# Two key loads on ScalarE's queue, a one-hot copy on GpSimd, and two more units masked by TensorE in a fused block-sparse attention and feed-forward kernel

## The chip, the cores and the metric

The kernel runs on one core of a Trainium2 chip. The metric is the device time of one execution in microseconds (us). Three runs of the kernel before gave 262.12, 262.63 and 263.25, with a median of 262.63. One further execution was recorded by the hardware profiler; it took 262.88, and its trace spans 261.1 from the first instruction to the last. All rows in this document that tell durations come from that one execution.

## The reference

Attention over 4 batches of 8 heads, 768 positions and a head width of 64, with a block mask, and then a feed-forward layer over all 3072 tokens. `rand_blocks` holds three drawn key blocks for each of the 24 query blocks, so the mask depends on an input (`sampled_blocks`) and has to be built on the chip.

```python
scores = scale * np.matmul(q, k.transpose(0, 1, 3, 2))
blk_i, blk_j = pos[:, None] // 32, pos[None, :] // 32
mask = np.abs(blk_i - blk_j) <= 1
mask = mask | (blk_i == 0) | (blk_j == 0) | (blk_i == 23) | (blk_j == 23)
for qb in range(24):
    for kb in sampled_blocks[qb]:
        mask[qb * 32:(qb + 1) * 32, kb * 32:(kb + 1) * 32] = True
scores = np.where(mask, scores, -1000000000.0)
attn = softmax(scores)                       # with a maximum taken off, and 1e-9 in the divisor
x = matmul(attn, v)  ->  (3072, 512)
h = x @ w_in                                 # 512 -> 2048
g = h * (1.0 / (1.0 + np.exp(-beta * h)))    # beta: one number for each of 2048
out = g @ w_out                              # 2048 -> 512
```

## The kernel before

**Units.** Two heads make a pair, so there are 16 pairs, 4 in each batch. A batch's 768 queries are cut into a tile of 256 and a tile of 512. A unit is one pair with one tile: units 0 to 3 are the four pairs of batch 0 with its first 256 queries, units 4 to 7 the same pairs with the other 512, and so on, 32 units in all. `tile_steps` cuts a unit into steps of 1024 scores for each partition: 3 steps where the tile has 256 queries, 6 where it has 512, 144 steps in the program. A step is a set of TensorE matmuls of `kX` (keys) by `qX` (queries) into a double PSUM bank `sc`, one ScalarE exponential of 128x1024 into a buffer `et`, and, for most units, one VectorE product of `et` with the 0/1 mask `mask01` (the function `mk`). Then follow the products with the values (`va`), a reciprocal and a scaling (`xst`), and a turn into `x`, the feed-forward's input.

**The mask.** The numbers of the drawn blocks are loaded into `sb_i32` by a DMA on ScalarE's queue. VectorE makes `mask16` of them (`mb`), one matmul spreads it over the query columns (`mt`), and ScalarE copies it to `mask_q` (`mtc`) and to `shut_qk` as 0 or -30000 (`neg`). Three more matmuls with the one-hot matrix `onehot` give `mask01` (`km`, `kmc`). For the first N_PEMASK = 4 units the mask is put on by TensorE: ahead of each pair of key-query matmuls stand two matmuls of `onehot` by `shut_qk` into the same bank, which put -30000 where a block is shut, and no VectorE product follows. In all other units VectorE multiplies.

**Loads.** Keys, queries and values come by SP's queue as fp32 into staging buffers (`st`, or parts of `g` early on), are cast to fp16 by VectorE or GpSimd (`s16`, `va`), and for batch 0 are turned by TensorE with the identity and copied to `kX` and `qX` by VectorE or ScalarE; later batches are turned by DMA. The keys of pairs 0 and 1 are loaded in parts (`IN_PARTS`), and `BESIDE` names one part that ScalarE's queue issues, behind `sb_i32`. GpSimd issues the loads of the weights, which also cast them.

**Feed-forward.** `hp` is x by w_in, `th` a tanh on ScalarE into `t_sb`, `gm` VectorE's product into `g`, then the output products with w_out. The first and the last 256 tokens and five tiles of 512 between them make seven stages; all but the first use sums and differences of `g` and `w_out` (tiles `s` and `w_mix`) that save one of eight block products.

**Order.** Nothing is scheduled when the kernel is built. Every operation becomes a node with a number, and the table `STEPS` lists all nodes in the order of their emission, each with its engine and its buffer slots; a colon joins two TensorE nodes that run as halves of the array. Each engine works through its own part of that list in order, so a wrong order shows as an engine that waits although other work is ready. Nearly all lines of the profile carry the line of one helper (`Tap.call`, L200), so groups are told apart by their tiles.

Of the kernel before, what the change touches and what calls it, by code (L numbers as in the profile page):

```python
# [11 lines left out]
FP16 = mybir.dt.float16  # L12
# [31 lines left out]
0D 1P0 3A 4P7 8P6 2A 5A 9A 35S4 31S0 32D0 36D1 39S 40D 41P5 49S1 65S4 13S1 33P6 37P1 34A2 42D 6P5  # L44
7A 38D 21S 17S3 25S 96P3 94P1 95Ae 50D1 66G6 14G2 92P0 22D 18G3 26G 45S0 55S2 23P4 15P2 16D1 24D
59S3 10S 43S5 97A0 27P3 19P5 20D 29S4 28A 46G5 53S6 93A1 51P2 80P2 84P3 67P0 47P3 81A3 56G5 73G
82P2 74G 48D0 52D 60D1 68D 57P1 58D3 85A2 44G0 83A5 108P1 109Ac 106P3 107A6 104P2 61P1 62D 30D2
105A4 98P1 99P 116P3 87P0:86 100D0 101D0 117A8 63S7 75G 76G 69S8 54D1 118P1 188P2 189A9 86P 88D4
89D3 120P3 70G6 77G 78G 110P0 111P 112D2 11P4 12D 113D4 64D3 121A1 90P6 197P2 119Aa 194P0 79G
122P1 123P 91D0 124D4 198A3 195Ab 125D3 71P7 72D 191P2 192Ae 114P2 203P0 212P3 213A0 200P2 115D  # L50
190D 196D 201A1 204Aa 215P1 102P7 103D 126P6 127D 214D 193D 199D 149P5 128P4 216Ac 150A2 129A5
137P0 205D 202D 138A0 131P1 140P2 134P3 146P7 143P6 130D1 151D 217D 227P2 141A3 135A1 147A4 144A6
148D 145D 136D 132A5 228A2 218P3 219A4 161P3 167P4 158P5 162A1 168A4 159A2 139D 133D 229D 142D
220D 163D 155P2 224P3 156A3 225Ad 206P0:207 169D 160D 221P2 157D 222A8 226D 207P 244P1 245Ab 208Da
223D 209D4 164P6 173P7 170P4 165A3 246D 152P5 250P0 166D 171A1 174A4 230P1:231 153A0 251A7 175D
247P3 248A6 231P 154D 236S2 239S5 240D0 172D 288P0 232D1 259P2 260A1 256P3 237G3 238S1 233D1 257Ae
242S6 241S 268S7 176P23:182 276P2 277A2 252D 182P 183P:177 279P2 289Ac 285P3 280A5 177P 178P:184
286A3 258D 261D 253P2 271S3 249D 278D 291P0 356D 254Aa 357D 360D 281D 290D 255D 274S8 300S0 282P3
184P 179P 210P4 185P 283A0 292A4 287D 284D 293D 262P0:263 269G1 358D 361D 359D 211A1 180A1 186A0
397P3 412P2 295P1:294 263P 264D3 265D4 398A8 413A9 403P3 294P 243G3 272G2 296D8 297D2 400P2 234P1  # L60
266P0 404Ad 298P2 401A4 235D 406P3 267A 409P2 270S0 303S4 306S1 407A1 299D 410A3 320P2 308P0 329P1
326P3 273S 304G4 311P7 309A3 301G3 402D 321A5 330A6 317P5 362D 405D 399D 363D 327A1 314P6 310D1
331D 322D 275G0 420S5 423S2 426S6 328D 312A0 318A5 319D 315A3 428P0 429A5 341P32:323 434P2 313D
435A6 421G2 323P 414D 316D 430D 411D 431P0 302S2 305S 181S 422S3 324A6 437P3 332P4 325D 335P5
432Aa 424G0 342A2 433D 350P2 333A4 343D 408D 436D 336A5 351A6 338P0 344P1 352D 337D 334D 438A2
339A3 443P1 444Ae 345A4 353P67:347 440P2 441A7 347P 354A1 415P1:416 364D0 445D 451P2 340D 452A0
346D 442D 348A3 439D 416P 454P2 457P0 455Ad 427G1 307G2 417D2 418D3 355D 349D 446P1:447 458Ab
463P2 447P 466P3 464A3 467A2 453D 367D 448Db 449D2 425S 460P0 373P4 461A4 480P1 486P3 370P5:374
487A1 474P0 374P 483P3 456D 465D 365D 459D 368D 462D 481Ac 468D 477P1 482D 475A8 478A7 484A5 371P
# [53 lines left out]
1289D 1181S 1180S 1294A0 1296D 1299P 1301P 1302A1 1300D 1297D 1298D 1303P 1304D 1305P 1306D 1313S  # L123
1312S 1307A 1311D 1308P 1309A 1314S
"""
N_PEMASK = 4
ROWS6 = False
N_XPE = 8
SHUT = 30000.0
# [3 lines left out]
BESIDE = ("k", 1, 2)  # L133
# [100 lines left out]
def kernel(  # L234
# [123 lines left out]
    def emit_first():  # L358
# [4 lines left out]
        for load in beside:  # L363
            load()
# [721 lines left out]
```

## Time and profile before

| | us |
|---|---|
| median of three runs | 262.63 |
| profiled execution, its own time | 262.88 |
| its span | 261.1 |
| TensorE busy | 249.6 (96%) |
| VectorE busy | 226.2 (87%) |
| ScalarE busy | 213.7 (82%) |
| GpSimd busy | 34.8 (13%) |

The span and the busy times come from the page's head. A busy TensorE is not TensorE at its peak: its matmuls are pipelined and the end of each is modelled, so a matmul's row is longer than the time until the next may start. The chain that ended last is counted back from the last instruction; where it names an engine, that engine's own work was what the end waited for. Idle time of an engine stands in brackets behind a row of the timeline, with what ended it.

### The profile page before, as it was taken

To read this page: it belongs to the slowest core of one execution; us is meant where nothing else is said; L and a number is where in the kernel's file an instruction comes from. 1 tells how busy PE (TensorE), PEld (TensorE's weight loads), DVE (VectorE), ACT (ScalarE), POOL (GpSimd) and SP (SyncE) were. 2 spreads that over 40 slices of the span, in tenths; PEclk is the share of its full clock that TensorE was granted. 3 is DMA by queue.
4 is the path that set the end of the run, shared out by engine and by line. 5 is a ranking of instruction groups with operands and counts; after the bars stand their busy time and mean duration, and the time that the engine had idled before them with its cause. 6 is when DMAs were issued, how large, how long until landed. Compare 5 with 4: busy or idle time off the path is not lost.

```text
span 261.1 us, 8802 instructions
## 1 busy us (share of the span) xinstructions
PE 249.6 (96%) x3767; PEld 171.8 (66%) x3767; DVE 226.2 (87%) x445; ACT 213.7 (82%) x288; POOL 34.8 (13%) x50
## 2 busy tenths in 40 slices
PE   5998799999989999999999999999999999999995
PEld 1675575564467976468876457856757986568894
DVE  4366998988999999989999999999999888589683
ACT  5699999999999997899898989975899874675241
POOL 3346001045220005210300200001100000000000
PEclk9999999999999999999999999999999999999999
DMA  6999994969756599931933999460050314100042
GB/s 202 340 342 175 207 198 85 280 167 262 178 194 189 175 121 246 172 133 35 261 83 73 251 147 253 57 137 0 3 183 4 22 23 173 22 3 0 3 160 81
DMA packets 50154, 36.81 MB, mean 141 GB/s; under 512 B 29748, under 2 KB 46660, under 8 KB 50116
## 3 DMA queue, kind: packets, MB, share of 16 engines
q1 hardware_dynamic: 46128, 31.80, 48.8%
q0 software_dynamic: 3680, 4.19, 9.8%
q8 instruction: 29, 0.48, 0.8%
q10 hardware_dynamic: 308, 0.26, 0.3%
q14 instruction: 9, 0.07, 0.1%
HBM read 27.27 MB, written 6.29 MB: 129 GB/s over the span
## 4 chain that ended last, share of the span: by engine, by line
PE 83%; DVE 11%; DMA 1%; ACT 1%; issue 1%; POOL 1%; SPq 0%; DVEq 0%; ACTq 0%
PE sc L200 83%; DVE et L200 5%; DVE g L200 3%; DMA st<-in_k_dram 1%; DVE xst L200 1%; ACT et L200 1%; DVE s L200 1%; DVE recip L200 0%; POOL s L200 0%; POOL va L200 0%; DVE kX L200 0%; ACT t_sb L200 0%; DVE va L200 0%; DVE x L200 0%; SPq L510 0%
## 5 line engine op out<-in xcount | busy, mean ns | idle before, releaser
L200 ACT ACTIVATE et<-sc 128x1024 f16<-128x1024 f32 x144 | 139.8, 1035 | 10.0 <-PE sc L200 8.5
L200 PE MATMUL sc<-x,w_in_sb 128*128 128x512 f16 (+2 forms) x504 | 92.1, 352 | 1.1 <-ACT et L200 0.5
L200 DVE TENSOR_TENSOR et<-et,mask 128x960 f16<-128x960 f16 x132 | 83.2, 670 | 1.4 <-ACT et L200 1.2
L200 ACT ACTIVATE t_sb<-sc,beta_c_sb 128x512 f16<-128x512 f32 (+1 forms) x112 | 65.1, 641 | 21.4 <-PE sc L200 19.4
L200 DVE SCALAR_TENSOR_TENSOR g<-t_sb,sc 128x512 f16<-128x512 f16 (+1 forms) x112 | 63.5, 606 | 7.8 <-ACT t_sb L200 7.3
L200 PEld LDWEIGHTS <-w_in_sb 128*128 128x128 f16 (+1 forms) x504 | 42.9, 97 | 37.5 <-issue 4.7
L200 PEld LDWEIGHTS <-g 64*128 64x128 f16 (+1 forms) x700 | 49.1, 96 | 15.2 <-issue 3.3
L200 PE MATMUL sc<-w_out_sb,g 64*128 64x256 f16 (+3 forms) x568 | 55.6, 281 | 0.5 <-DVE xst L200 0.3
L200 PE MATMUL sc<-qX,kX 64*128 64x256 f16 (+1 forms) x384 | 50.6, 328 | 1.4 <-DVE g L200 0.8
L200 PEld LDWEIGHTS <-et 64*128 64x128 f16 (+1 forms) x1776 | 41.7, 95 | 8.6 <-issue 1.4
L200 PE MATMUL sc<-va,et 64*128 64x65 f16 (+1 forms) x1776 | 44.3, 191 | 0.8 <-DVE xst L200 0.3
L200 PEld LDWEIGHTS <-kX 64*128 64x128 f16 x384 | 19.7, 95 | 12.5 <-issue 7.5
L200 POOL CAST s<-st 128x768 f16<-128x768 f32 (+2 forms) x17 | 15.1, 905 | 87.4 <-PE sc L200 34.5
L200 PEld LDWEIGHTS <-s 64*128 64x128 f16 (+1 forms) x320 | 22.0, 97 | 6.0 <-issue 1.7
L200 PE MATMUL sc<-w_mix,s 64*128 64x256 f16 (+1 forms) x272 | 23.6, 270 | 0.0
L200 DVE TENSOR_TENSOR xst<-sc,recip 128x256 f16<-128x256 f32 (+1 forms) x32 | 17.8, 557 | 0.9
L200 POOL CAST va<-st 128x768 f16<-128x768 f32 x10 | 9.6, 968 | 59.0 <-DVE g L200 32.0
L200 ACT COPY osb<-sc 128x512 f32<-128x512 f32 (+3 forms) x19 | 10.0, 539 | 8.5 <-PE sc L200 7.5
L200 PE MATMUL sc<-w_mix,g 64*128 64x256 f16 (+3 forms) x128 | 15.6, 264 | 0.0
L200 DVE TENSOR_TENSOR osb<-osb,sc 128x512 f32<-128x512 f32 (+2 forms) x19 | 11.7, 618 | 2.6 <-PE sc L200 1.5
L200 DVE RECIPROCAL recip<-sc 128x4 f32<-128x4 f32 (+1 forms) x32 | 6.2, 193 | 8.0 <-PE sc L200 7.7
L200 DVE CAST s<-st 128x768 f16<-128x768 f32 (+2 forms) x15 | 7.7, 522 | 2.0 <-DMA st<-in_k_dram 2.0
(60 smaller groups left out, 94.8 us busy)
## 6 DMA issues: line engine op xcount, KB each, us to landing
out_dram<-osb SPq DMA_DIRECT2D x23, 256.0 KB, 2.4
st<-in_k_dram SPq DMA_DIRECT2D x12, 384.0 KB, 4.9
st<-in_q_dram SPq DMA_DIRECT2D x12, 384.0 KB, 5.1
st<-in_v_dram SPq DMA_DIRECT2D x12, 384.0 KB, 4.5
g<-in_v_dram SPq DMA_DIRECT2D x4, 384.0 KB, 6.9
w_in_sb<-in_moe_w_in_dram POOLq DMA_DIRECT2D x2, 512.0 KB, 7.1
w_in_sb<-in_moe_w_in_dram POOLq DMA_DIRECT2D x1, 1024.0 KB, 10.7
w_out_sb<-in_moe_w_out_dram POOLq DMA_DIRECT2D x2, 512.0 KB, 12.9
```

The costliest lines, as they stand in the source:

```text
L200: r = f(*a, **kw)
```

## The change

Four things are changed by hand, and then `STEPS` is replaced as a whole.

First, `BESIDE` now names two loads, the first third of the keys of pair 1 and of pair 0. ScalarE's queue issues the one of pair 1 ahead of `sb_i32` and the one of pair 0 behind it; SP issues the rest of both. Pair 0's keys come in two parts where there were three. Second, the re-ordered copy `onehot` moves from ScalarE to GpSimd. Third, units 4 and 5 are masked by TensorE as units 0 to 3 are: `shut_qk` becomes 384 columns wide where it was 128, and lies in the buffer `s`, which the feed-forward needs only later. Each of the 12 steps of these units gets two matmuls of 64 rows and 512 columns, and loses VectorE's product. Fourth, the remaining queries of a pair (`rest_of`) use the pair's first staging buffer.

```diff
-N_PEMASK = 4
+PE_MASKED = {0: 6, 1: 6, 2: 6, 3: 6, 4: 6, 5: 6}
...
-BESIDE = ("k", 1, 2)
+BESIDE = (("k", 1, 0), ("k", 0, 0))
...
-IN_PARTS = {0: (0, 2, 4, 6), 1: (0, 2, 6)}
+IN_PARTS = {0: (0, 2, 6), 1: (0, 2, 6)}
...
-    shut_qk = persist.tile([P, P], FP16, name="shut_qk")
+    shut_qk = T["s"][0].rearrange("p a f q -> p (a f q)")[:, 0:NG * P]
...
+        beside[0]()
         nc.scalar.dma_start(out=sb_i32, in_=sb_lo)
-        for load in beside:
-            load()
+        for i in range(1, len(BESIDE)):
+            beside[i]()
...
+        nc.gpsimd.tensor_copy(out=onehot, in_=onehot_n.rearrange("b p g -> b g p"))
         nc.gpsimd.tensor_copy(out=ident32, in_=identity[0:16, 0:16])
...
-        nc.scalar.copy(out=onehot, in_=onehot_n.rearrange("b p g -> b g p"))
...
-                act.activation(out=shut_qk, in_=at(tb)[:, 0:P], func=AF.Copy, bias=-SHUT,
+                act.activation(out=shut_qk, in_=at(tb)[:, 0:NG * P], func=AF.Copy, bias=-SHUT,
                                scale=SHUT)
...
+        if nm == "q":
+            st, more = rest_of.setdefault(x, st), lo > 0
...
+            by_pe = len(steps) < n_by_pe
...
-                                rhs=shut_qk[r].unsqueeze(1).to_broadcast([D, CG, P]),
+                                rhs=shut_qk[r, q0 // CG:(q0 + n) // CG].rearrange(
+                                    "b (g p) -> b g p", p=P).unsqueeze(1).to_broadcast(
+                                        [D, CG, ng, P]),
...
-            steps, ets = tile_steps(x, q0, n, i * NPAIR + j < N_PEMASK)
+            steps, ets = tile_steps(x, q0, n, PE_MASKED.get(i * NPAIR + j, 0))
...
-0D 1P0 3A 4P7 8P6 2A 5A 9A 35S4 31S0 32D0 36D1 39S 40D 41P5 49S1 65S4 13S1 33P6 37P1 34A2 42D 6P5
+31S4 27S0 35S 0D 32G3 28D2 13S1 1P0 3A 17S3 36D 18G0 33P7 29P1 2A 14D1 30A3 34A 45S1 21S 41S0 51S2
```

What the new table does to the engines' queues is shown at three places. The first is the head of ScalarE's queue, from its first DMA to its second exponential; `st_0` is the staging of pair 1's keys, `sc_3_64` and the like are PSUM double banks, `et_14` and `et_0` take the exponentials of pair 1's first two steps. Before:

```order
L362 DMA sb_i32_158<-in_sampled_blocks_dram 24x6
L510 DMA st_0_130<-in_k_dram 128x2x256
L392 ACT_TABLE_LOAD
L392 COPY onehot_153<-g_1_111 128x384
L200 CAST mask_q_156<-sc_0_61 24x384
L200 ACTIVATE shut_qk_154<-sc_0_61 128x128
L200 CAST mask01_157<-sc_3_64 128x384 x2
L200 COPY kX_2_126<-sc_3_64 128x256
L200 CAST mask01_157<-sc_2_63 128x384
L200 ACTIVATE et_14_79<-sc_1_62 128x1024
L200 ACTIVATE et_0_65<-sc_3_64 128x1024
L200 COPY kX_1_124<-sc_1_62 128x256
```

The same place in the changed kernel, where `s_0_117` is the new home of `shut_qk`:

```order
L509 DMA st_0_130<-in_k_dram 128x2x128
L362 DMA sb_i32_157<-in_sampled_blocks_dram 24x6
L509 DMA st_1_131<-in_k_dram 128x2x128
L199 ACT_TABLE_LOAD
L199 CAST mask_q_155<-sc_0_61 24x384
L199 ACTIVATE s_0_117<-sc_0_61 128x384
L199 COPY kX_3_128<-sc_0_61 128x256
L199 COPY qX_3_129<-sc_3_64 128x256
L199 COPY kX_3_128<-sc_3_64 128x512
L199 ACTIVATE et_14_79<-sc_0_61 128x1024
L199 ACTIVATE et_0_65<-sc_2_63 128x1024
L199 COPY qX_2_127<-sc_3_64 128x768
```

The load of `sb_i32` stands one DMA later, the one-hot copy and the three copies to `mask01` have left ScalarE, and all three copies that pair 1's first steps need are on it. Before, the first exponential in the queue took `sc_1_62`, which TensorE fills second; now it takes the bank that TensorE fills first.

The second place is VectorE's queue where the feed-forward's first products (`g`) begin, while units 4 and 5 are on their way. Before:

```order
L200 TENSOR_TENSOR et_9_74<-et_9_74,mask01_157 128x8x120
L200 TENSOR_TENSOR et_11_76<-et_11_76,mask01_157 128x8x120
L200 COPY x_0_114<-sc_3_64 128x256 x2
L200 TENSOR_TENSOR et_0_65<-et_0_65,mask01_157 128x8x120
L200 TENSOR_TENSOR et_14_79<-et_14_79,mask01_157 128x8x120
L200 TENSOR_TENSOR et_3_68<-et_3_68,mask01_157 128x8x120
L200 TENSOR_TENSOR et_10_75<-et_10_75,mask01_157 128x8x120
L200 TENSOR_TENSOR et_1_66<-et_1_66,mask01_157 128x8x120
L200 SCALAR_TENSOR_TENSOR g_1_111<-t_sb_5_108,sc_2_63 128x256
```

The changed kernel at the same copies to `x`:

```order
L199 COPY x_0_114<-sc_3_64 128x256 x2
L199 SCALAR_TENSOR_TENSOR g_0_110<-t_sb_2_105,sc_2_63 128x256
L199 SCALAR_TENSOR_TENSOR g_0_110<-t_sb_0_103,sc_2_63 128x256
L199 SCALAR_TENSOR_TENSOR g_0_110<-t_sb_1_104,sc_3_64 128x256
L199 SCALAR_TENSOR_TENSOR g_0_110<-t_sb_5_108,sc_3_64 128x256
```

The seven mask products that stood ahead of the first `g` are gone; the first mask product comes only after sixteen `g`.

The third place is TensorE's queue at the first step of unit 4. Before, two matmuls fill the double bank:

```order
L200 LDWEIGHTS kX_1_124
L200 MATMUL sc_2_63<-qX_1_125,kX_1_124 128x512
L200 LDWEIGHTS kX_1_124
L200 MATMUL sc_2_63<-qX_1_125,kX_1_124 128x512
L200 LDWEIGHTS et_3_68
```

In the changed kernel two of the mask stand ahead of them:

```order
L199 LDWEIGHTS onehot_153
L199 MATMUL sc_3_64<-s_0_117,onehot_153 128x512
L199 LDWEIGHTS onehot_153
L199 MATMUL sc_3_64<-s_0_117,onehot_153 128x512
L199 LDWEIGHTS kX_0_122
L199 MATMUL sc_3_64<-qX_0_123,kX_0_122 128x512
```

So a step of units 4 and 5 has four matmuls of 512 columns where it had two.

Over the whole program, ScalarE's queue of exponentials and tanhs keeps its pattern: 20 exponentials with one copy among them, 8 tanhs, 2, 4, 3 and 4, 11 exponentials, in both. VectorE has 120 mask products for 132, 8 casts of 768 columns for 13, 3 copies to `mask01` for none, and 19 copies of 512 columns to the output staging for 22. GpSimd has 5 more casts of 768 columns and the one-hot copy, and ScalarE 3 more copies of 512 columns to the output staging.

More of the change, by code (lines that the diff above doesn't have):

```diff
@@ L49 @@
[L49 to L54, printed above, removed]
@@ L132 @@
 GATE = "q3"
[L133 to L135 removed]
+BESIDE = (("k", 1, 0), ("k", 0, 0))
+COPY384 = {"ACT": 395, "DVE": 465}
+EARLY = ("k2", "q2", "k3", "q3", "v0", "v1", "v2", "v3")
 SLACK = 1500
@@ L459, in add_mask @@
                        rows=32)
-            mask_of[g] = add("mask", ("ACT", "DVE", "POOL"), COPY384, 100,
+            mask_of[g] = add("mask", ("ACT", "DVE"), COPY384, 100,
                              lambda eng, g=g, kb=kb: kmc(eng, g, kb), deps=[n_km], use=[kb])
```

193 lines of the change are left out of this document (100 added, 93 removed).

## The prediction

> **What bounds the kernel now.** I read the page's head and its chain first, then the busy time by stage, then the opening in order of time. The chain says that TensorE sets most of the end and VectorE a ninth of it:
>
> ```profile
> span 261.1 us, 8802 instructions
> PE 83%; DVE 11%; DMA 1%; ACT 1%; issue 1%; POOL 1%; SPq 0%; DVEq 0%; ACTq 0%
> ```
>
> An average over stages hides who sets the pace in each. The next rows give, for each stretch, its length and the busy time of TensorE, its weight loads, VectorE, ScalarE and GpSimd:
>
> ```profile
> 0.00:12.00 12.00, 8.85 (x58) 4.51 (x60) 5.41 (x24) 6.69 (x12) 4.10 (x17) 1.00 0.85 261
> 12.00:26.00 14.00, 12.72 (x239) 9.37 (x235) 8.51 (x23) 13.76 (x15) 7.79 (x11) 1.00 1.10 268
> 26.00:80.00 54.00, 50.85 (x886) 30.12 (x887) 49.73 (x98) 52.52 (x75) 10.92 (x11) 1.00 0.87 192
> 80.00:120.00 40.00, 39.38 (x610) 27.81 (x605) 38.81 (x70) 36.02 (x45) 5.89 (x6) 1.00 0.74 168
> 120.00:200.00 80.00, 79.88 (x1258) 54.45 (x1257) 77.50 (x140) 70.39 (x88) 6.07 (x6) 1.00 0.54 121
> ```
>
> From 12 to 80 us the engine that is never free is ScalarE: 66.28 of 68, so it idles 1.7 us there. TensorE idles 4.4 us in the same time (1.28 and 3.15), VectorE 9.8. From 80 to 200 TensorE is full (0.7 us idle), with VectorE at 97%. So there are three stages: an opening of 12 us in which everybody waits for loads and the mask, 68 us at the pace of the exponentials, and the rest at TensorE's pace. A microsecond saved in the opening moves the exponentials forward by one, and through them what follows. Work given to TensorE before 80 us can lie in its 4.4 us; VectorE's relief matters where TensorE waits for VectorE.
>
> The opening in order of time (start, length, engine, what; in brackets the idle time before and its end):
>
> ```profile
> 0.74 0.66 ACTq L362 DMA_DIRECT2D sb_i<-in_sampled_blocks_dram  x1
> 1.26 0.45 SPq L510 DMA_DIRECT2D st<-in_k_dram  x1
> 1.42 0.41 ACTq L510 DMA_DIRECT2D st<-in_k_dram  x1
> 2.25 0.16 DVE L200 CAST sb_f<-sb_i 24x3 f32<-24x3 int32 x1 [0.21 <-DMA sb_i<-in_sampled_blocks_dram]
> 3.32 0.50 PE L200 MATMUL sc<-g,mask 24*128 24x384 f16 x1 [0.24 <-DVE mask L200]
> 3.85 0.47 ACT L200 CAST mask_q<-sc 24x384 f16<-24x384 f32 x1 [0.18 <-PE sc L200]
> 4.22 0.26 ACT L200 ACTIVATE shut_qk<-sc 128x128 f16<-128x128 f32 x1
> 4.37 0.79 PE L200 MATMUL sc<-mask_q,onehot 24*128 24x384 f16 x2 [0.56 <-ACT mask_q L200]
> 4.88 0.86 ACT L200 CAST mask<-sc 128x384 f16<-128x384 f32 x2 [0.39 <-PE sc L200]
> 5.12 0.83 DVE L200 CAST s<-st 128x256 f16<-128x256 f32 x3 [1.86 <-DMA st<-in_k_dram]
> 6.00 1.03 PE L200 MATMUL sc<-identity,s 128*128 128x128 f16 x8 [0.84 <-DVE s L200]
> 7.53 0.40 PE L200 MATMUL sc<-shut_qk,onehot 64*128 64x256 f16 x2
> 8.36 0.42 PE L200 MATMUL sc<-shut_qk,onehot 64*128 64x256 f16 x2
> 9.46 1.94 ACT L200 ACTIVATE et<-sc 128x1024 f16<-128x1024 f32 x2 [1.34 <-PE sc L200]
> 11.40 0.37 ACT L200 COPY kX<-sc 128x256 f16<-128x256 f16 x1
> 11.67 3.78 ACT L200 ACTIVATE et<-sc 128x1024 f16<-128x1024 f32 x4
> ```
>
> The first scores start at 7.53 and the second step's at 8.36, four pairs later, so a pair follows another by 0.21 and the first bank is full at 8.36 - 0.21 + 0.42 = 8.57. Yet ScalarE sits idle for 1.34 us until 9.46, because its queue asks for the second bank first. After two exponentials and a copy the third starts at 11.67, and from there ScalarE runs on.
>
> **The change, part by part.** The prices of the small copies (busy time, mean ns of one):
>
> ```profile
> L200 ACT COPY x<-sc 128x512 f16<-128x512 f16 x3 | 1.8, 591 | 0.0
> L200 ACT COPY kX<-sc 128x256 f16<-128x256 f16 x2 | 0.7, 372 | 1.1 <-PE sc L200 1.1
> L200 ACT CAST mask<-sc 128x384 f16<-128x384 f32 x3 | 1.3, 481 | 0.8 <-PE sc L200 0.8
> L392 ACT COPY onehot<-g 128x384 f16<-128x384 f16 x1 | 0.5, 511 | 0.0
> L378 POOL COPY g<-identity 64x384 f16<-64x384 f16 x2 | 1.0, 500 | 0.1
> ```
>
> First the opening. ScalarE's queue issues a key load ahead of `sb_i32`, so the drawn blocks start one issue later: 0.41 at least. How long its 24 short rows then stand behind 128 KB of keys no row tells; the nearest is the keys that SP issued at 1.26, whose cast waited until 5.12, while the small load alone took from 0.74 to 2.25. I take the blocks at 2.7 to 3.4, 0.5 to 1.1 later; beyond that lies a rival below. From there the rows of before give the chain: 2.25 to 3.85 is 1.60 to `mask_q`, and 0.5 more to its use by TensorE at 4.37 (2.1 after the blocks). The changed queue of TensorE has three matmuls for `mask01` next (0.79 for two, so 1.1), then six turns of keys (8 in 1.03, so 0.75), and then the first scores: 2.7 + 2.1 + 1.1 + 0.75 = 6.7, or 7.4 for the late end. On ScalarE the wider `shut_qk` costs 0.22 more (0.48 as the 384-column cast of the mask, where 128 columns took 0.26) and the first two copies 0.37 each; that path is ready at 2.7 + 1.60 + 0.37 + 0.48 + 0.74 = 5.9, before TensorE. The key loads need to be there by the turns at about 6; before they were at 5.12, with three casts of 0.83 in all. The first bank takes 1.03 (7.53 to 8.57), so the first exponential starts at 7.7 to 8.4, and the third after 1.94 of exponentials and a copy of 768 columns. 256 columns more cost 0.22, so 768 cost 0.81, of which 0.1 overlaps with the next as it did at 11.40. The third exponential comes at 7.7 + 1.94 + 0.7 = 10.3 to 11.0, where it came at 11.67: 0.7 to 1.4 gained, and I take **-1.0**. The later loads of batch 0 leave SP in nearly the same order with one DMA less ahead of them, and before they kept ScalarE waiting for only 0.24 us from 12 to 26.
>
> The one-hot copy costs GpSimd about 0.5, as its copies of 384 columns do, right behind them at 2.8; ScalarE is spared 0.51 at 3.16, while it was waiting for the mask anyway (`mask_q` at 3.85). Zero on both sides. It covers itself only as long as GpSimd's next cast waits for a load; without that cover the first turn of queries would come up to 0.5 late, ahead of scores that wait for the mask chain still longer. The three copies to `mask01`, 0.48 each on ScalarE, go to VectorE in the opening, where it is 45% busy: zero.
>
> Then the masks. Twelve steps get two matmuls of 64 rows and 512 columns; the two run side by side in the halves of the array, as those of the scores do:
>
> ```profile
> 39.97 0.37 PE L200 MATMUL sc<-qX,kX 64*128 64x512 f16 x2
> 41.02 0.84 PE L200 MATMUL sc<-qX,kX 64*128 64x512 f16 x6
> L200 DVE TENSOR_TENSOR et<-et,mask 128x960 f16<-128x960 f16 x132 | 83.2, 670 | 1.4 <-ACT et L200 1.2
> ```
>
> Two pairs more are 0.84 - 0.37 = 0.47, so a pair is 0.235 and twelve are **2.8 us of TensorE**. They belong to exponentials 13 to 24, which at 0.97 each behind the third start between about 20 and 34 us, in the stage where ScalarE sets the pace and TensorE has 4.4 us idle. A step then needs 0.47 of TensorE for 0.97 of ScalarE. I take 0, with 2.8 as the upper end: if they do not find the idle time, all of it shows.
>
> VectorE loses 12 x 0.670 = 8.0 us there, and its queue from there on is short. In the exponentials' stage that gains nothing by itself, as ScalarE had 1.7 us idle. Later it can only give what TensorE waits for. TensorE's visible idle time from 12 to 200 us is 5.2 (4.4 and 0.7); 2.8 of it is filled by the new matmuls, so 2.4 is the most; no less than 0. I take a third, **-0.8**, being nearest to the 0.7 that TensorE idles after 80 us. Five casts that go to GpSimd take some more off VectorE:
>
> ```profile
> L200 POOL CAST s<-st 128x768 f16<-128x768 f32 x13 | 13.4, 1040 | 82.5 <-PE sc L200 34.5 <-DVE s L200 22.6 <-DVE recip L200 17.7
> L200 POOL CAST s<-g 128x768 f16<-128x768 f32 x2 | 1.7, 827 | 3.1 <-DMA g<-in_k_dram 2.1 <-issue 1.0
> ```
>
> GpSimd sat idle 82.5 us ahead of such casts, so it has room; a cast there takes 1.04 beside a busy VectorE and 0.83 early on, and that 0.2 is all that a row shows of one engine in the other's way. The Trainium skill ("SBUF — State Buffer", section "Who interferes with whom") says that VectorE, in its two-port modes or with two inputs from SBUF, and GpSimd take a shared port pair as a lock, so that the second blocks fully until the first is done. By that, five casts of 1.04 could hold VectorE up by 5.2 of the 8.0 us it is relieved of, and the term would shrink from -0.8 to -0.3; the trace agrees in direction with its 0.2.
>
> The new order is the part that no row prices. The places where an order goes wrong are seen on the chain of before:
>
> ```profile
> 12.60 1.02 issue
> 74.84 0.84 POOL va L200
> ```
>
> Each is a wait of about 1 us that another order might have spared or may bring. I take 0 and keep 1.0 on either side.
>
> The sum: -1.0 + 0 - 0.8 + 0 = -1.8 us, so a span of 259.3. The profiled execution took 262.88, 1.8 over its span, so 261.1; the median of the runs shown lies 0.25 below that execution. I forecast **260.8**, 0.7% under the median of 262.63. A half per cent, 1.3 us, is about what a measurement of this kernel can tell from no change: faster is below 261.3, slower above 263.9. The bounds (opening 0.3 up and 0.4 down, VectorE 0.8 up and 1.6 down, order 1.0 either way) don't fall together; the root of their squares is 1.3 up and 1.9 down, so the forecast's own range is 258.9 to 262.1.
>
> **The rivals.** *TensorE was the bound all along (slower).* The chain names it for 83% of the span, and it executes in order, so idle time in small pieces need not be there for a given matmul to use. Then the 2.8 us are paid in full; the opening gives back 1.0 at most and VectorE nothing, and a misplaced wait of 1.0 can come on top: 264.4, or 265.4 with the wait. It decides if less than about 1 us of the 4.4 before 80 us can be filled. For it speaks the share of the chain; against it, that ScalarE is 97% busy there. Chance 0.16.
>
> *The mask chain is late (no change).* The drawn blocks now wait behind a key load. If they arrive 1.9 us later or more, at 4.1, the first exponential is at 2.1 + 1.85 + 1.03 behind it, 9.1, the third at 11.7, and the opening gives nothing: 261.8. The keys at 1.26 needed 3.9 us to their cast, so this is within reach. The Trainium skill ("DMA: Bandwidth & Descriptors", section "Issuing engines are not separate DMA queues") speaks for it: loads of all queues end up on the same 16 DMA engines and interleave, and a second queue saves the issue time alone. By that rule the keys come sooner by one issue at most, 0.45 us by SP's row. No row of before contradicts it: the two key loads issued at 1.26 and 1.42 on two queues were cast together at 5.12. Chance 0.19.
>
> *VectorE held TensorE up (much faster).* It is 97% busy from 80 to 200, and the chain gives it 11% of the span, 29 us. If its queue is what delays `g` and the scaled values, 8 us less work gives the full 2.4 and spares the order some waits: -1.0 - 2.4 - 1.0 is 258.2. Against it: TensorE is visibly idle for 0.7 us in those 120. Chance 0.17.
>
> **How the numbers follow.** The forecast has 0.48, the rivals 0.16, 0.19 and 0.17. Faster: four fifths of the forecast's 0.48 (0.38), the third rival whole (0.17), and a fifth of the late mask (0.04), together 0.59. Slower: 0.12 of the first rival, 0.02 of the late mask and 0.02 of the forecast, 0.16. The rest, 0.25, is the same. The range of eight in ten goes from 257.9, a little under the third rival, to 264.4, the first rival without its extra wait; what is left out is the half of that rival that also waits, and smaller tails.
>
> **What would show it.** In the changed profile: the first exponential at 7.7 to 8.4 us and the third at 10.3 to 11.0; the cast of the drawn blocks at 2.7 to 3.4; ScalarE full from there to 80 us, with under 2.5 us idle; 72 matmuls of `onehot` by `s`, 24 of them 512 wide, with TensorE's busy time between 12 and 80 us up by 2 to 3 and no new wait of TensorE before them; VectorE's busy time down by 8 or more. I am wrong in the opening if the third exponential is at 11.5 or later, wrong about the cover if ScalarE waits for TensorE while units 4 and 5 run, and wrong about VectorE if its relief shows as shorter waits of TensorE worth over 2.4 us.

## The result and the profile after

The changed kernel takes 265.91 us (four runs, 265.38 to 265.94) where the kernel before takes 262.73 beside it (262.12 to 263.25). The ratio is 1.0117, with a 95% interval of 1.0092 to 1.0143: 3.2 us slower by the medians, where 1.8 us faster was forecast. The profiled execution is one of the four; its span is 264.1 us, 3.0 more than before. Head of the page and its chain of the end, after the change:

```profile
span 264.1 us, 8832 instructions
PE 86%; DVE 6%; ACT 4%; issue 1%; DMA 1%; POOL 0%; ACTq 0%; DVEq 0%
```

VectorE's share of the chain fell from 11 to 6%, and the time went up all the same. The opening shows where. Rows of the timeline, of several engines, in order of time:

```profile
1.25 0.72 ACTq L362 DMA_DIRECT2D sb_i<-in_sampled_blocks_dram  x1
3.99 0.16 DVE L199 CAST sb_f<-sb_i 24x3 f32<-24x3 int32 x1 [1.94 <-DMA sb_i<-in_sampled_blocks_dram]
5.37 0.47 ACT L199 CAST mask_q<-sc 24x384 f16<-24x384 f32 x1 [1.66 <-PE sc L199]
5.89 0.29 DVE L199 CAST s<-st 128x256 f16<-128x256 f32 x1 [0.58 <-DMA st<-in_k_dram]
8.00 0.40 PE L199 MATMUL sc<-s,onehot 64*128 64x256 f16 x2
8.13 0.83 POOL L199 CAST s<-g 128x768 f16<-128x768 f32 x1 [2.14 <-PE sc L199]
9.07 1.94 ACT L199 ACTIVATE et<-sc 128x1024 f16<-128x1024 f32 x2 [0.39 <-PE sc L199]
9.82 1.46 PE L199 MATMUL sc<-identity,s 128*128 128x128 f16 x12
10.98 0.83 POOL L199 CAST s<-g 128x768 f16<-128x768 f32 x1 [1.46 <-PE sc L199]
11.21 0.40 PE L199 MATMUL sc<-s,onehot 64*128 64x256 f16 x2
11.82 0.39 PE L199 MATMUL sc<-qX,kX 64*128 64x256 f16 x2
12.58 0.51 PE L199 MATMUL sc<-identity,s 128*128 128x128 f16 x6
13.13 0.56 DVE L199 COPY kX<-sc 128x768 f16<-128x768 f16 x1 [0.65 <-PE sc L199]
13.72 0.80 ACT L199 COPY qX<-sc 128x768 f16<-128x768 f16 x1 [2.71 <-DVE kX L199]
14.42 1.95 ACT L199 ACTIVATE et<-sc 128x1024 f16<-128x1024 f32 x2
15.50 0.40 PE L199 MATMUL sc<-s,onehot 64*128 64x256 f16 x2 [1.86 <-ACT et L199]
15.66 0.45 PE L199 MATMUL sc<-qX,kX 64*128 64x256 f16 x2
15.88 0.45 PE L199 MATMUL sc<-s,onehot 64*128 64x256 f16 x2
```

The drawn blocks are cast at 3.99 instead of 2.25, and the first exponential starts at 9.07. It is still 0.39 us earlier than before. Then ScalarE's queue holds the copy of pair 2's queries (node 48 of the order table) ahead of the third exponential. That copy waits 2.71 us, and not for its own input. Pair 2's queries are cast at 8.13 and turned in the group of twelve that starts at 9.82; their turn was over by 10.98, for there GpSimd's cast of the keys starts, which waits for TensorE and takes the same buffer (slot 2 in the table's entries 46G2 and 42G2). What the profile names as the copy's releaser is VectorE's copy of pair 2's keys: it ends at 13.13 + 0.56 = 13.69, and the copy starts 0.03 later. That interval is 0.03 in two more traces with the same queue; what in the program orders the two copies was not followed up. The keys' copy in turn waits for their turn (12.58). Their cast had ended at 10.98 + 0.83 = 11.81, but the turn stands in TensorE's queue behind the scores of the third and the fourth exponential, from 11.21 on. The scores of the third exponential were complete at 11.82 + 0.39 = 12.21; it starts at 14.42, 2.75 us later than before (11.67). With ScalarE late TensorE finds no free bank and stands too, 1.86 us up to 15.50, and then its pairs follow each other by 0.2 us again, where they had come down to 0.11 before the pause. Of the stretches of the prediction, after the change (length; busy time of TensorE, weight loads, VectorE, ScalarE, GpSimd; granted clock, DMA share, GB/s):

```profile
12.00:26.00 14.00, 11.95 (x187) 8.95 (x182) 6.31 (x16) 11.58 (x13) 8.03 (x11) 0.88 1.12 242
26.00:80.00 54.00, 52.78 (x858) 31.01 (x856) 44.08 (x88) 52.23 (x75) 9.07 (x10) 1.00 0.81 179
120.00:200.00 80.00, 79.66 (x1347) 53.77 (x1346) 75.37 (x134) 70.44 (x91) 9.89 (x9) 1.00 0.54 125
```

From 12 to 26 us ScalarE is idle for 2.4 us (0.24 before) and TensorE's granted clock is 0.88 (1.00 before). Counted along the trace, the 49th exponential starts at 75.83 us (73.71 before, so 2.1 late), the 97th at 139.73 (3.05 late), and the last tanh ends at 253.67 (3.2 late). The loss is there by the third exponential; what comes after gives back 0.6 us by the 49th and loses it again, with 0.5 more by the end.

### The profile page after: what moved, and what is told of

The parts are those of the page before. It is cut to its first block, busy times and chain, and to the rows that moved or that the text cites. A ratio compares the mean times of both kernels' runs of the same rounds, so it can differ in the third digit from the quotient of the medians.

```text
span 264.1 us, 8832 instructions
## 1 busy us (share of the span) xinstructions
PE 253.3 (96%) x3783; PEld 173.2 (66%) x3783; DVE 218.0 (83%) x425; ACT 213.9 (81%) x289; POOL 40.0 (15%) x55
## 4 chain that ended last, share of the span: by engine, by line
PE 86%; DVE 6%; ACT 4%; issue 1%; DMA 1%; POOL 0%; ACTq 0%; DVEq 0%
PE sc L199 86%; ACT et L199 3%; DVE g L199 2%; DVE et L199 2%; ACT t_sb L199 1%; DMA sb_i<-in_sampled_blocks_dram 1%; DVE xst L199 1%; DVE osb L199 0%; ACT qX L199 0%; POOL s L199 0%; DVE kX L199 0%; ACTq L509 0%; DVE qX L199 0%; DVE recip L199 0%; DVE mask L199 0%
## 5 line engine op out<-in xcount | busy, mean ns | idle before, releaser
L199 DVE TENSOR_TENSOR et<-et,mask 128x960 f16<-128x960 f16 x120 | 76.4, 674 | 1.5 <-ACT et L199 1.5
L199 PE MATMUL sc<-w_out_sb,g 64*128 64x256 f16 (+2 forms) x576 | 55.7, 282 | 0.2 <-ACT et L199 0.2
L199 PE MATMUL sc<-qX,kX 64*128 64x512 f16 (+1 forms) x384 | 52.0, 332 | 0.4 <-DVE g L199 0.2
L199 POOL CAST s<-st 128x768 f16<-128x768 f32 (+2 forms) x21 | 19.5, 943 | 90.0 <-DVE et L199 35.4
L199 PEld LDWEIGHTS <-kX 64*128 64x128 f16 x384 | 20.3, 97 | 10.6 <-issue 5.1
L199 PE MATMUL sc<-w_mix,s 64*128 64x256 f16 (+1 forms) x272 | 23.7, 270 | 0.0
L199 ACT COPY osb<-sc 128x512 f32<-128x512 f32 (+3 forms) x23 | 12.2, 536 | 8.3 <-PE sc L199 7.3
L199 DVE TENSOR_TENSOR osb<-osb,sc 128x512 f32<-128x512 f32 (+2 forms) x19 | 11.7, 617 | 7.0 <-issue 2.5
L199 DVE RECIPROCAL recip<-sc 128x4 f32<-128x4 f32 (+1 forms) x32 | 6.2, 192 | 10.3 <-PE sc L199 9.9
L199 PE MATMUL sc<-s,onehot 64*128 64x256 f16 (+1 forms) x72 | 12.5, 354 | 2.1 <-ACT et L199 1.9
```

What stands on the lines that cost most here:

```text
L199: r = f(*a, **kw)
```

## The experiments

Theory: the copy of pair 2's queries, waiting in ScalarE's queue, holds the third exponential, and with it everything. Rivals: the late drawn blocks are the loss; or TensorE pays for the added mask matmuls. Four kernels tell them apart. "Of before" below is the ratio to the kernel before, run beside each.

**Only the copy moved.** In the order table, node 48 goes from ScalarE to VectorE, behind pair 2's key copy:

```diff
-43P7 44D2 62D5 76P1 69G 70G 71G 48A 91A8
+43P7 44D2 48D 62D5 76P1 69G 70G 71G 91A8
```

> The changed kernel with one copy moved: the 128x768 copy of pair 2's queries (qX) leaves ScalarE's queue, where it stands ahead of the third exponential, and stands on VectorE behind pair 2's key copy. My theory (the copy, which waits for GpSimd's cast of pair 2's keys and VectorE's copy of them, holds the third exponential from about 12.25 to 14.42 us, and all that follows runs parallel): third exponential at 12.2 to 12.6, last tanh about 2 us earlier, time about 263.9 (263.2 to 264.6). Rival, the late drawn blocks alone cost the 3 us (first exponential 9.07 and what is behind it): time unchanged, 265.9. Rival, TensorE pays for the 24 added mask matmuls in full and is the bound: a freer ScalarE gives nothing, 265.5 or more.

Measured: 262.38 us, 1.0003 of before (0.9983 to 1.0023). ScalarE in its opening:

```profile
9.46 1.94 ACT L199 ACTIVATE et<-sc 128x1024 f16<-128x1024 f32 x2 [0.39 <-PE sc L199]
12.63 3.77 ACT L199 ACTIVATE et<-sc 128x1024 f16<-128x1024 f32 x4 [1.24 <-PE sc L199]
```

The third exponential comes at 12.63, 1.79 earlier, although the blocks came at 4.37 in this execution. (On VectorE the copy still stands behind that of the keys, but no exponential stands behind it.) One copy on another engine is worth 1.14% or 3.0 us, nearly the whole loss; more than the 2 us expected. The rest of it fits TensorE's clock, by the next run.

**Only the drawn blocks first.** ScalarE's queue issues `sb_i32` ahead of both key loads:

```diff
-        beside[0]()
         nc.scalar.dma_start(out=sb_i32, in_=sb_lo)
-        for i in range(1, len(BESIDE)):
+        for i in range(len(BESIDE)):
             beside[i]()
```

> The changed kernel with the drawn block numbers issued first on ScalarE's queue again, ahead of both key loads. My theory: the blocks are cast at about 2.3 instead of 3.99 and the first two exponentials come earlier (first at 7.4 to 8.4), but the third still stands behind the copy of pair 2's queries and starts at about 14.4: time unchanged within 0.6 us, 265.3 to 266.2. Rival, the late drawn blocks are the whole loss: the third exponential comes 1.7 us earlier, at 12.7, and the time is 264.2 or less. Rival, TensorE is the bound: unchanged, and unchanged also when the copy is moved.

Measured: 264.31 us, 1.0073 of before (1.0047 to 1.0099). VectorE's cast of the blocks, and ScalarE:

```profile
2.23 0.16 DVE L199 CAST sb_f<-sb_i 24x3 f32<-24x3 int32 x1 [0.19 <-DMA sb_i<-in_sampled_blocks_dram]
8.62 1.94 ACT L199 ACTIVATE et<-sc 128x1024 f16<-128x1024 f32 x2 [0.39 <-PE sc L199]
13.11 0.80 ACT L199 COPY qX<-sc 128x768 f16<-128x768 f16 x1 [2.56 <-DVE kX L199]
13.81 2.86 ACT L199 ACTIVATE et<-sc 128x1024 f16<-128x1024 f32 x3
```

The blocks come 1.76 earlier, the first exponential only 0.45 (the scores then wait for key casts that stand at 5.04), and the third 0.61. The copy waits nearly as long as it did. So the late blocks are not the loss, though "unchanged within 0.6" was a miss too: 1.2 us were gained. The six executions suggest why. Three with a mean granted clock of 1.0 took 263.61 to 263.90; three with 0.994 took 264.72 to 265.62. All four of the changed kernel are at 0.991 to 0.994. One stretch at the lower clock goes with about 1.2 us (between the middle ones, 263.68 and 264.87), and half of these executions escape it. That it lies behind the pause is seen in the changed kernel's trace alone; of the other executions only the mean is known.

**Both.**

> Both edits together: the drawn block numbers issued first, and the copy of pair 2's queries on VectorE. My theory: first exponential at 7.4 to 8.4, third at 10.3 to 11.8 where it came at 14.42, so 2.6 to 4 us less: 262 to 263.3. If the two costs were independent of each other, the gain is the sum of the two single edits' gains; my theory says it is more than that sum, since the blocks gain nothing alone. Rival, TensorE pays 2.8 us for the added mask matmuls: not under 264.5 whatever the third exponential does.

Measured: 261.97 us, 0.9984 of before (0.9959 to 1.0009), no difference from it. ScalarE, and TensorE's third step:

```profile
8.56 1.94 ACT L199 ACTIVATE et<-sc 128x1024 f16<-128x1024 f32 x2 [0.39 <-PE sc L199]
9.30 1.46 PE L199 MATMUL sc<-identity,s 128*128 128x128 f16 x12
10.70 0.40 PE L199 MATMUL sc<-s,onehot 64*128 64x256 f16 x2
11.77 4.69 ACT L199 ACTIVATE et<-sc 128x1024 f16<-128x1024 f32 x5 [1.27 <-PE sc L199]
```

The two edits together take off 3.5 us, less than the sum of the two alone (3.0 and 1.2), not more: that part of the expectation fell. The sizes fit one account: copy 1.79 and clock 1.2 are 3.0; blocks 0.61 and half of 1.2 are 1.2; both, 14.42 - 11.77 = 2.65 and 1.2 are 3.85, for 3.5 measured. The fit is a loose one: with this order of the opening the third exponential stands at 11.03 to 12.04 in five traces (this one, the three runs on the masks that start from it, and the one that moves the one-hot copy). With the third exponential back at 11.77 (11.67 before), the time is back as well. TensorE had not been the bound: the rival's 264.5 is excluded.

The late blocks were then put into the kernel before, alone:

```diff
-        nc.scalar.dma_start(out=sb_i32, in_=sb_lo)
         for load in beside:
             load()
+        nc.scalar.dma_start(out=sb_i32, in_=sb_lo)
```

> The kernel before with one thing changed: ScalarE's queue issues its key load ahead of the load of the drawn block numbers. By what the changed kernel showed (blocks cast at 3.99 behind such a load where 2.25 stood): blocks cast at 3.9 to 4.4, the mask matmuls hold TensorE's turns back to about 7, first exponential at 10.4 to 11.2 where it came at 9.46, third about 1.0 to 1.6 later, time 263.4 to 264.2. Rival, as the prediction put it (0.5 to 1.1 later, at 2.7 to 3.4): under 0.4 us, 262.4 to 262.8, since the keys' cast at 5.12 is later than the mask then needs.

Measured: 264.89 us, 1.0082 of before (1.0056 to 1.0108). Its blocks and its exponentials:

```profile
4.45 0.16 DVE L200 CAST sb_f<-sb_i 24x3 f32<-24x3 int32 x1 [2.40 <-DMA sb_i<-in_sampled_blocks_dram]
10.64 1.94 ACT L200 ACTIVATE et<-sc 128x1024 f16<-128x1024 f32 x2 [1.34 <-PE sc L200]
12.84 3.96 ACT L200 ACTIVATE et<-sc 128x1024 f16<-128x1024 f32 x4
```

The same swap delays the blocks by 2.2 us here and the first exponential by 1.18. By itself, where no copy hides it, the swap costs 2.2 us, more than expected: the third exponential is 1.17 late, the ninth 1.5 (18.93 for 17.42), the 49th 1.6 and the 97th 2.4 (139.08 for 136.68); what delays the later ones further was not followed up.

**The masks.** Units 4 and 5 back on VectorE, each product right behind its exponential:

```diff
-PE_MASKED = {0: 6, 1: 6, 2: 6, 3: 6, 4: 6, 5: 6}
+PE_MASKED = {0: 6, 1: 6, 2: 6, 3: 6}
...
+            def ex_mk(eng):
+                ex(eng)
+                mk("DVE")
...
```

> The changed kernel with units 4 and 5 masked by VectorE again: the 24 mask matmuls are gone and 12 products of 128x960 stand on VectorE, each right behind its exponential; the order is otherwise the changed kernel's. My theory (the matmuls lie in TensorE's idle time, ScalarE sets the pace there): time unchanged within 0.7 us, 265.2 to 266.6, third exponential still at 14.4. Rival, TensorE pays in full: 2.8 us less, 263.1. Rival, VectorE is the limit there: slower by 1 to 4 us.

Measured: 276.52 us, 1.054 of before (1.0515 to 1.0566), outside every expectation. VectorE while the two units run, and then the stretch from 26 to 80 us:

```profile
28.83 0.66 DVE L200 TENSOR_TENSOR et<-et,mask 128x960 f16<-128x960 f16 x1 [2.66 <-ACT et L200]
31.79 0.66 DVE L200 TENSOR_TENSOR et<-et,mask 128x960 f16<-128x960 f16 x1 [1.23 <-ACT et L200]
47.38 0.66 DVE L200 TENSOR_TENSOR et<-et,mask 128x960 f16<-128x960 f16 x1 [2.60 <-ACT et L200]
```

```profile
26.00:80.00 54.00, 46.64 (x670) 28.25 (x668) 39.41 (x82) 42.20 (x59) 3.75 (x5) 0.85 0.67 149
```

Each product stands at the head of VectorE's queue until its exponential is done, and what TensorE needs from VectorE stands behind it; TensorE falls idle and its clock to 0.85. This run tells of the place of the products, not of the price of the masks. Three others tell that, all of them the version with both edits. Without any mask on the two units (`n` is 512 in these and 256 in units 0 to 3):

```diff
-                        if by_pe:
+                        if by_pe and n < 512:
...
-                            start=not by_pe, stop=True)
+                            start=not (by_pe and n < 512), stop=True)
```

> The version with both edits (blocks first, copy on VectorE; 261.97 us in the last runs), with the 24 mask matmuls of units 4 and 5 left out: neither TensorE nor VectorE masks these two units. My theory (the matmuls lie in idle time of TensorE while ScalarE sets the pace): 261.3 to 262.4, no gain over 0.5 us. Rival, TensorE pays them in full: 2.8 us less, 259.2; if half, 260.6.

With their mask matmuls doubled:

```diff
-                    for hh in range(2):
+                    for hh in range(2 * max(1, n // 256) if by_pe else 0):
+                        hh, again = hh % 2, hh // 2
                         if by_pe:
...
-                                start=True, stop=False)
+                                start=again == 0, stop=False)
```

> The version with both edits (261.97 us), with the mask matmuls of units 4 and 5 done twice, 24 more of 64 rows and 512 columns, 2.8 us of TensorE by the price of the prediction. My theory: a step then needs 0.94 of TensorE (0.47 and twice 0.235) for 0.97 of ScalarE, with products of values and the first feed-forward work beside it, so the idle time of 4 us before 80 us is used up and part of it shows: 262.3 to 264.0. Rival, all idle time is still to be used: 262.0. Rival, paid in full: 264.8.

With VectorE's products behind the second-next exponential:

```diff
-PE_MASKED = {0: 6, 1: 6, 2: 6, 3: 6, 4: 6, 5: 6}
+PE_MASKED = {0: 6, 1: 6, 2: 6, 3: 6}
...
+            def ex_mk(eng):
+                ex(eng)
+                WAITING.append(mk)
+                if len(WAITING) > 2:
+                    WAITING.pop(0)("DVE")
...
```

> The version with both edits (blocks first, copy on VectorE; 0.9984 of the kernel before), with units 4 and 5 masked by VectorE as in the kernel before, each product placed in VectorE's queue behind the second-next exponential of these units, so that VectorE doesn't wait for the exponential that has just been issued (the earlier try had each product right behind its own exponential and came out at 1.054). Theory from the runs without masks (about 1 us cheaper) and with masks twice (2.9 dearer): moving the masks to TensorE costs 0 to 1 us and VectorE's relief gives nothing, so this comes out 0 to 1 us faster than the version with both edits, 0.995 to 0.999 of the kernel before. Rival, VectorE's relief is worth the 0.8 us of the prediction: 1.001 to 1.005. Rival, products still hold VectorE's queue up ahead of what TensorE needs: over 1.01.

Measured: 261.13 us without masks, 0.9946 of before (0.9925 to 0.9966); 264.91 with the matmuls doubled, 1.0093 (1.0069 to 1.0116); 261.42 with VectorE's products, 0.9946 (0.9913 to 0.9978). Against 0.9984 the first 24 matmuls cost 1.0 us and the next 24 cost 2.9, which is their whole price of 2.8: TensorE's idle time takes one set and not two. For the second set the rival came true, not the expectation. The traces agree: from the third exponential to the 24th, which starts behind the last of these matmuls, it takes 23.7 us without masks, 23.9 with one set and 26.3 with two. The last of the three is the version that beats both kernels. Its stretch, and that of the version with both edits:

```profile
26.00:80.00 54.00, 51.72 (x815) 31.25 (x816) 50.83 (x98) 52.81 (x75) 8.99 (x10) 1.00 0.81 190
```

```profile
26.00:80.00 54.00, 53.13 (x833) 31.66 (x833) 46.74 (x92) 52.96 (x75) 8.99 (x10) 1.00 0.82 191
```

VectorE has 4 us more to do there and ScalarE is as full as ever. The run without masks and the one with the products differ by VectorE's twelve products alone, and both are at 0.9946: its relief shows no gain, though the two intervals together would hide one of up to 1.0 us. The 1.0 us of the masks is near what can be told apart too (the interval of 0.9984 overlaps with both of 0.9946), and the traces don't put it where the masks are: from the third exponential to the 49th it takes 60.01 us with the mask matmuls, 60.16 without masks, 60.36 with the products. What differs there comes later and is told in the last section.

**The one-hot copy** back on ScalarE, in the version with both edits:

```diff
-        nc.gpsimd.tensor_copy(out=onehot, in_=onehot_n.rearrange("b p g -> b g p"))
...
+        nc.scalar.copy(out=onehot, in_=onehot_n.rearrange("b p g -> b g p"))
```

> The version with both edits, with the re-ordered one-hot copy back on ScalarE (0.51 us there, behind the activation table's load). Theory: ScalarE waits for the mask chain anyway and GpSimd's first key cast, which stands right behind the copy at 3.46, has its result used at 3.91 and by work that waits for the mask: no change, 0.996 to 1.001 of the kernel before. Rival, GpSimd's copy delays the casts and turns of the opening: 0.3 to 0.5 us faster, 0.996 to 0.997.

Measured: 262.11 us, 0.997 of before (0.9945 to 0.9994), the same as 0.9984 within the intervals: no difference seen, as forecast, though the rival's 0.3 us is too small to be excluded.

**Can the opening be shorter?** In the version with both edits the third exponential waits 1.27 us for its scores. They go into the bank that the second exponential reads until 8.56 + 1.94 = 10.50, and TensorE is at twelve turns until 10.7; it begins them at 10.70. First try: the third step into a free bank, pair 2's turns later.

```diff
-46G2 5D 16D0 9D 38A 92P2 55S3 10S 65S 89Ae 19P2 47P6 93A0 22G 23P1 42G2 24D 20D 7D 90P2 80P0 52G4 39S5 43P7 44D2 48D 62D5 76P1 69G 70G 71G 91A8
+5D 16D0 9D 38A 46G2 22G 92P2 7D 55S3 10S 65S 89Ae 42G3 90P1 93A0 91A8 19P7 23P0 20D 24D 43P6 44D2 80P0 47P7 48D 76P1 52G4 39S5 62D5 69G 70G 71G
```

> The version with both edits (261.97 us), with the order of the opening changed by hand: the third step of pair 1 goes into a free double bank, ahead of the turns of pairs 0 and 2, so that it does not wait for the second exponential to read its bank; pair 2's key cast takes a free buffer; pair 2's turns come last. Theory, ScalarE sets the pace from its third exponential to 80 us: third exponential at 10.5 where it came at 11.77, fourth at 11.8 or before, sixth or so 0.5 to 1.1 us earlier than in the version with both edits, and the time 260.9 to 261.5, which beats the kernel before. Rival, the time lies with TensorE from 80 us on and it does not start earlier: 262.0. Rival, the fourth exponential now waits as long as the third did: 261.8 to 262.2.

Measured: 262.55 us, 0.9997 of before (0.9980 to 1.0014). ScalarE:

```profile
8.95 2.85 ACT L199 ACTIVATE et<-sc 128x1024 f16<-128x1024 f32 x3 [0.39 <-PE sc L199]
12.60 6.59 ACT L199 ACTIVATE et<-sc 128x1024 f16<-128x1024 f32 x7 [0.80 <-PE sc L199]
```

The third no longer waits, and the fourth does, as the second rival had it. A second order put pair 0's turns and steps ahead of pair 2's as well (the banks of eight later nodes change with it):

```diff
-46G2 5D 16D0 9D 38A 92P2 55S3 10S 65S 89Ae 19P2 47P6 93A0 22G 23P1 42G2 24D 20D 7D 90P2 80P0 52G4 39S5 43P7 44D2 48D 62D5 76P1 69G 70G 71G 91A8 25S4 104P2
+22G 5D 16D0 9D 38A 46G2 7D 19P7 20D 92P2 55S3 10S 65S 89Ae 42G3 23P3 24D 90P3 93A0 91A8 80P0 76P1 81A1 43P5 44D2 47P4 48D 77A2 78P3 79Ad 52G4 39S5 62D5 69G 70G 71G 25S4 104P0
```

> The version with both edits, with the opening's order changed by hand so that neither the third nor the fourth exponential waits: the third step of pair 1 goes into a free double bank right behind the second, pair 0's turns of queries and remaining keys stand ahead of it, pair 0's two steps follow, and pair 2's turns come behind those. Theory, ScalarE sets the pace from its first exponential to 80 us: exponentials one behind the other from 8.6 us on, the sixth at 13.4 to 14.0 where it came at 14.65, and the time 0.6 to 1.2 us less than the version with both edits: 0.993 to 0.996 of the kernel before, which beats it. Rival, the time from 26 us on is set by TensorE, which is 98% busy there, so that a fuller ScalarE gives nothing: 0.998 to 1.000.

Measured: 264.27 us, 1.0061 of before (1.0041 to 1.0081): slower, with the sixth exponential at 14.30 (14.50 in the version with both edits). The cause was sought on GpSimd, whose fourth key cast had been listed behind VectorE's copies. One entry moved:

```diff
-42G3 23P3 24D ... 79Ad 52G4 39S5
+42G3 52G4 23P3 24D ... 79Ad 39S5
```

> The opening without gaps (1.0061 of the kernel before) with one entry moved: GpSimd's fourth key cast, of pair 3, is emitted ahead of pair 0's last turn instead of behind pair 2's copies. A GpSimd cast is made to wait for the VectorE operation emitted ahead of it, so in the last run it waited 4.09 us for VectorE's copy of pair 2's queries, and the weight loads and value casts of GpSimd's queue came some 2 us later than in the version with both edits (0.9984). Theory: that wait is the whole loss; GpSimd's cast starts at 10.5 to 12, the first value cast about 2 us earlier, and the time falls to 0.996 to 0.999 of the kernel before. Rival, the loss is TensorE's colder start in that order: no change, 1.004 to 1.008.

Measured: 262.53 us, 0.9995 of before (0.9982 to 1.0008). GpSimd's casts in the second order, and then with the entry moved:

```profile
14.51 0.96 POOL L199 CAST s<-g 128x768 f16<-128x768 f32 x1 [4.09 <-DVE qX L199]
```

```profile
8.61 2.40 POOL L199 CAST s<-g 128x768 f16<-128x768 f32 x3
```

That one wait was the 1.7 us. Without it the second order is no better than the first: its third exponential starts at 11.35, since TensorE, still at its half pace and with the turns in between, delivers the second step's scores 0.27 and the third's 0.48 us late. The fuller opening is lost again further on. Against the version with both edits the 13th exponential is 0.2 us earlier (21.02 for 21.22), the 24th 0.8 later (36.52 for 35.70) and the 49th 1.8 later (73.59 for 71.78). Why stays open.

## Why the prediction was wrong

**The opening, -1.0, came out at about +3.** Two of its steps failed. The drawn blocks were put at 2.7 to 3.4; they came at 3.99 (4.37 in another execution of the same queue). That is just short of the late-mask rival's condition, 4.1, and its first exponential, 9.1, came true at 9.07. What the forecast put behind the blocks was right: the first scores start 4.01 us after them (3.99 to 8.00), where it had 2.1 + 1.1 + 0.75 = 3.95. The rule quoted with that rival from the Trainium skill ("DMA: Bandwidth & Descriptors", section "Issuing engines are not separate DMA queues"), that a second queue saves the issue alone, is not contradicted: pair 1's key cast starts at 4.71, right behind VectorE's work on the mask and without a wait, 0.41 sooner than before (5.12), and how much sooner the keys had come is not seen. But that rival let the third exponential come at 11.7.

The larger failure is the step "7.7 + 1.94 + 0.7": the copy of 768 columns was priced by its length, 0.7, without its own wait. It was the 12th row of the queue that the text on the change shows, with `qX_2` in its name, and by the trace it starts only when pair 2's keys have been loaded, cast, turned and copied. The wait measured 2.71 and its removal 3.0 us. The lower clock behind the pause, about 1.2 of the 3.0, was in no term. And the same step took the third step's scores for ready: they use the bank of the second exponential, stand behind twelve turns and need 0.6 to 1.0 us of TensorE themselves, so that without any copy ahead of it the third exponential comes at 11.03 to 12.04, not at 10.3 to 11.0. Which it is depends on TensorE's pace: the third follows the first by 2.64 us in the two traces in which the third step's pairs are 0.11 apart, and by 3.21 in the three in which they are still 0.21 apart. Against 11.67 before, an order of that kind had 0.6 us to win there at best in these traces.

**The masks at 0** held as far as the 49th exponential; over the whole program they cost 0 to 1.0, within the stated 0 to 2.8. The cover was named rightly, its size was not: 4.4 us of idle time would have taken 1.6 of the second set's 2.8, and that set was paid in full.

**VectorE at -0.8** was not borne out. By the forecast the masks' move, at 0 for TensorE and -0.8 for VectorE, gains 0.8 us; taken back, with 4 us of products on VectorE again in that stage, it made the kernel 1.0 us faster and not 0.8 slower (0.9946 for 0.9984, with an upper end of 0.9978). The 9.8 us that VectorE idled from 12 to 80 had said so; the third of 2.4 was an allowance without a row. Whether GpSimd's casts held VectorE up by the port pair that the prediction quotes from the Trainium skill can't be told from this, since its relief showed no gain either way.

**The one-hot copy at 0** was right. **The order at 0, with 1.0 either way:** with both edits the whole change is at -0.4 us with its third exponential at +0.1, and with the copy moved alone it is at +0.1 with the third exponential at +1.0. So the rest of the order was worth about 0.5 to 0.9 us and inside its bounds; the misplaced copy, which was part of that order, was not.

**The rivals.** TensorE as the bound gave 264.4, and the time was near it for another reason: its extra matmuls were not what was paid. VectorE holding TensorE up, at 2.4 us, is excluded by the run with the products. The rival that was missing is the one that the trace shows, a copy ahead of an exponential in an in-order queue, with a wait that runs over three other engines.

## What to carry to other kernels

An instruction in an in-order queue costs its own wait, not its length: for each instruction that a new order puts ahead of a critical one, follow what it waits for back to the load before pricing it, its inputs and also what else the program orders ahead of it, and ask which bank the critical one's input has to share. Here a pause of under 2 us at the start was paid twice, once as delay and once, by all that the runs show, as TensorE's clock.

## What the runs showed of the hardware

**A short pause can cost the clock.** TensorE's pause of 1.86 us was followed by pairs 0.2 us apart instead of 0.11. Two windows of the changed kernel, the first with the pause (13.6 to 15.50) and the second behind it; the columns are those of the stretches above:

```profile
12.05:15.46 3.41, 1.58 (x24) 1.04 (x21) 1.79 (x4) 1.74 (x3) 2.61 (x4) 1.00 1.06 370
15.46:18.87 3.41, 3.37 (x31) 2.59 (x31) 0.00 (x0) 3.41 (x4) 3.08 (x5) 0.50 1.08 181
```

The clock is halved for 3.41 us, and 0.5 x 3.41 of 264.1 is just what a mean of 0.994 lacks. With the blocks first the profiled execution shows the same pause of 1.86 and no fall, and so does the run with each product behind its exponential (15.85); three executions of six with the blocks first have the lower mean, at 1.2 us each. The pause is not the only way to it: 3 of the 78 executions of the kernel before that ran beside the experiments have 0.994 as well, at 264.61 to 265.28. The ten runs whose traces have no pause of 1.86 us in the opening have it in none of 94. The Trainium skill ("TensorE: Matmul & The Clock Gate", section "What's actually happening") gives an idle window of about 3.4 us for the fall, counted by a window that runs freely. The length of the stretch and the dependence on luck agree; a pause of about half that length was enough here, with TensorE busy for 1.58 of the 3.41 us ahead of the fall, and the measurement decides.

**A few bytes behind a key load.** The drawn blocks, 24 short rows, issued 0.51 us later (1.25 for 0.74), were usable 1.74 later.

**TensorE stops at fixed counts of its instructions.** Groups of value products are broken up by an idle time that no wait explains. The timeline of the changed kernel, then its window up to the second stop (`x` counts matmuls and weight loads), then the queue of instruction packets on its page:

```profile
55.66 0.80 PE L199 MATMUL sc<-va,et 64*128 64x65 f16 x40 [0.58 <-issue]
94.45 0.38 PE L199 MATMUL sc<-va,et 64*128 64x65 f16 x13 [0.53 <-issue]
```

```profile
0.00:94.44 94.44, 87.16 (x1372) 55.41 (x1373) 69.11 (x150) 83.11 (x110) 24.30 (x40) 0.98 0.88 210
```

```profile
q8 instruction: 29, 0.48, 0.7%
```

The same two views of the version with both edits:

```profile
90.50 0.38 PE L199 MATMUL sc<-va,et 64*128 64x65 f16 x13 [0.62 <-issue]
```

```profile
0.00:90.49 90.49, 85.70 (x1372) 54.31 (x1373) 70.36 (x151) 82.36 (x109) 23.88 (x40) 1.00 0.90 220
```

The stop is behind the same 1372 matmuls in both, and also with the one-hot copy on ScalarE (1.16 us) and with the doubled masks, whose 24 more matmuls lie ahead of it: it goes with the count of instructions, not with the work. The changed kernel's first stop is behind 735 matmuls and 735 loads, 1275 instructions ahead of the second, which is close to five times 256; the one stop of the kernel before (0.15 us at 39.36) is behind 479 and 479, exactly twice 256 ahead of that first one. The packets are of about 0.48 MB / 29 = 16.6 KB. The Trainium skill ("Runtime: NRT & Kernel Launch", section "Instruction fetch mechanics") says that code is refilled in blocks of 16 KiB, 256 instructions, mostly hidden. Size and spacing agree; that these stops are such refills, late beside the loads, fits but was not tested. Nor is it known what lets one show: the runs without mask matmuls on units 4 and 5 and the one with only the copy moved have no stop of that kind at 1372. In the changed kernel the second stop, 0.53 us, falls between the 49th exponential and the 97th, where it lost 0.9 again of what it had gained back; in the profiled execution of the version with both edits the one stop is 0.62, beside the 1.0 us that the masks seemed to cost.
